# A list order for all of layer 1, and layer 2's first operands summed in DRAM by accumulating transfers

## The chip, the cores and the metric

The kernel runs on one core of a Trainium2 chip. The metric is the device time of one execution in microseconds (us). TensorE multiplies matrices, VectorE and ScalarE do elementwise work, SyncE (SP) issues transfers, and GpSimd (POOL) is idle in the kernel before.

## The reference

Attention with two local masks, then two feed-forward layers over 2304 tokens, all in float32:

```python
scores = np.where(masks, scale * q @ k.T, -1e9)          # 8 heads of 64; heads 4 to 7 dilated by 4
attn = softmax(scores) @ v                               # window of 32 keys, [4, 8, 576, 64]
x = attn.transpose(0, 2, 1, 3).reshape(2304, 512)
h = x @ w_in                                             # layer 1: 512 -> 2048 -> 512
P = a[0] + a[1] * h + a[2] * h**2 + a[3] * h**3
Q = 1 + abs(b[0]) * abs(h) + abs(b[1]) * h**2
y = (P / (Q + 1e-6)) @ w_out
h = y @ w2_in                                            # layer 2: 512 -> 2048 -> 512
out = (max(h, 0) + alpha * min(h, 0)) @ w2_out
```

## The kernel before

**Tiling.** Features lie on partitions. The tokens go in six blocks of 384. In layer 1 a pair `J` (0 to 47, eight to a block) is two chunks of 128 hidden features for one block: `inproj` forms two chunks of `h` in the two PSUM banks `h` (line 645), `rat_1` and `rat_2` evaluate P / Q (lines 663 to 677), `g_split` splits the result into a high part and a low part (lines 684 and 685), and `outproj1` two pairs later multiplies by `w_out` (line 695) and adds up in the banks `y0` to `y3`. Past the first block a product is three matmuls of float32r parts, high times high, high times low and low times high, each of 384 columns. At a block's end `y` goes through a tile `os` to DRAM (`y_dram[block, m]`, m of four groups of 128 features).

**Attention.** A unit `U` (four to a block, the last two dilated) is two heads of one block: scores into banks `aS` and `aP`, a maximum, exponentials (line 512), normalization (line 532), transposes, a copy `pts`, and the product with `v` into a bank `h` (line 582), which is copied as `xh` (line 609) and gives the low part `xl` (line 615). Past the first four, one unit runs in two pairs.

**Layer 2** works on two blocks at a time with seven products in place of eight (Strassen and Winograd). For a block pair, with B11, B21 the first and B12, B22 the second block's halves of y, it needs seven right operands: B11, B21, B22 and T1 = B12 - B11, T3 = B22 - B12, T2 = B22 - T1, T4 = B21 - T2. `x_load` fetches y from DRAM, `x_combine` takes the four differences on VectorE (line 760), and `x_place` splits each operand into a high part on ScalarE (line 742) and a low part on VectorE (line 743). `st_prep` forms and splits the weights' combinations (`st_a`, `st_s`). `product` (line 836) multiplies in the order B11, T2, B21, T3, T4, T1, B22 for each of eight pairs of chunks; `v` and `u` (lines 871 and 866) are the first copies and sums out of the banks. `outproj2` (line 714) gives the output. For the first block pair `x_load(0)` is written at pair 43, `x_combine(0)` and the first `x_place` at 44, and the others at 45 to 47 and behind.

**Weights** arrive as 64-bit numbers and are converted (`w_convert`: ScalarE line 375, VectorE 381 to 396). `w_early` converts eleven tiles of layer 2's during pairs 16 to 42 and writes them back to DRAM (`w_dram`).

**The order.** At its end the program hands all instructions of TensorE, VectorE, ScalarE and SP to `in_order_of_need`. It projects start times with a table of costs, picks on each engine the ready instruction with the longest way to the end, and chains those that it places before `ORDERED`; the rest are left to the framework's scheduler, behind the last chained one:

```python
if start < ORDERED:
    order[e].append(k)
...
rest = [(k, ks[-1]) for k in range(n) if todo[k].engine == e and k not in chosen]
```

`ORDERED` is 115e3 ns, about the first eight pairs. SP stays in written order.

## Time and profile before

| what | us |
|---|---|
| median of 3 runs | 887.02 |
| lowest and highest | 885.96, 888.42 |
| profiled execution, its own time | 887.51 |
| its span, first to last instruction | 885.7 |

The profile is of one execution. Its page gives busy times by engine, the span in slices, the chain of waits that ended last and groups of instructions. The trace behind it answers by stretch of time, by line, and as a timeline. The granted clock of TensorE is 1.0, the upper of its two levels (2.4 GHz), over the whole span. In a timeline the ends of matmuls are modelled and overlap, so starts are compared. A bracket at the end of a row gives the idle time of the engine just before it, and what ended that.

### The profile page before, as it was taken

The numbers are of one execution on the slowest core, as the hardware profiler recorded it, in microseconds if no ns is written. First come the engines' busy times: TensorE is split into PE (matmuls) and PEld (weight loads), VectorE is DVE, ScalarE is ACT, GpSimd is POOL, SyncE is SP. The second block draws the span as 40 slices with busy tenths as digits, with TensorE's granted clock in tenths as the row PEclk, the third lists the DMA queues.
The fourth block names the chain that finished last, engine by engine and source line by source line (L and its number), as shares of the span: only waits on it lengthen the run. The fifth ranks groups of instructions, "written<-read, shape, count | busy, mean of one in ns | idle before, by whom it ended". The sixth has DMA issues, their size and how long they took to land.

```text
span 885.7 us, 14822 instructions
## 1 busy us (share of the span) xinstructions
PE 872.5 (99%) x5746; PEld 779.0 (88%) x5746; DVE 760.7 (86%) x1199; ACT 613.3 (69%) x1253; POOL 0.2 (0%) x4
## 2 busy tenths in 40 slices
PE   9999999999999999999999999999999999999997
PEld 6555678999999999999999999898888989899896
DVE  5999999999999998988899999998986778767652
ACT  6999988788877888887677576557554456635423
POOL 0000000000000000000000000000000000000000
PEclk9999999999999999999999999999999999999999
DMA  9964212133334434440021242323320011210001
GB/s 346 407 238 176 82 57 79 38 115 140 130 109 139 173 125 148 160 149 19 20 78 42 95 131 95 119 79 119 101 85 24 27 46 60 97 47 25 1 0 72
DMA packets 32903, 92.78 MB, mean 105 GB/s; under 512 B 3905, under 2 KB 11329, under 8 KB 32833
## 3 DMA queue, kind: packets, MB, share of 16 engines
q1 hardware_dynamic: 32832, 91.83, 29.9%
q8 instruction: 45, 0.74, 0.3%
q14 instruction: 26, 0.20, 0.1%
HBM read 76.61 MB, written 15.20 MB: 104 GB/s over the span
## 4 chain that ended last, share of the span: by engine, by line
PE 57%; ACT 18%; DVE 18%; DMA 4%; issue 2%; SPq 0%; ACTq 0%
PE ps_h L836 19%; PE ps_y L714 14%; PE ps_y L695 9%; PE ps_h L645 7%; PE ps_aS L714 4%; PE ps_aP L714 3%; ACT p L512 3%; DVE tb L675 2%; DVE tc L676 2%; ACT p L532 2%; ACT tc L664 2%; ACT ta L673 2%; DVE tc L677 2%; ACT ta L674 2%; ACT ta L663 1%
## 5 line engine op out<-in xcount | busy, mean ns | idle before, releaser
L645 PE MATMUL ps_h<-xh,winh 128*128 128x384 f32 x320 | 110.4, 345 | 2.7 <-DVE tc L666 2.2
L695 PE MATMUL ps_y<-gh,wouth 128*128 128x384 f32 x320 | 108.4, 339 | 0.0
L695 PE MATMUL ps_y<-gl,wouth 128*128 128x384 f32 x320 | 107.1, 335 | 0.3 <-DVE gl L685 0.3
L695 PE MATMUL ps_y<-gh,woutl 128*128 128x384 f32 x320 | 107.2, 335 | 0.0
L645 PE MATMUL ps_h<-xh,winl 128*128 128x384 f32 x320 | 107.2, 335 | 0.0
L645 PE MATMUL ps_h<-xl,winh 128*128 128x384 f32 x320 | 107.1, 335 | 0.0
L714 PE MATMUL ps_y<-wouth,gl 128*128 128x512 f32 x192 | 74.9, 390 | 0.0
L714 PE MATMUL ps_y<-woutl,gh 128*128 128x512 f32 x192 | 74.9, 390 | 0.0
L714 PE MATMUL ps_y<-wouth,gh 128*128 128x512 f32 x192 | 74.8, 390 | 0.0
L663 ACT ACTIVATE ta<-ps_h,root 128x384 f32<-128x384 f32 x96 | 57.3, 596 | 18.7 <-PE ps_h L645 18.4
L664 ACT ACTIVATE tc<-ps_h,co 128x384 f32<-128x384 f32 x96 | 66.5, 694 | 0.0
L645 PEld LDWEIGHTS ps_h<-xh,winh 128*128 128x128 f32 x320 | 60.0, 188 | 6.9 <-DVE tc L666 3.7
L742 ACT ACTIVATE gh<-tc 128x768 fp32r<-128x768 f32 x48 | 40.3, 841 | 30.5 <-PE ps_aP L714 28.0
L695 PEld LDWEIGHTS ps_y<-gl,wouth 128*128 128x128 f32 x320 | 60.2, 188 | 0.6 <-DVE gl L685 0.6
L645 PEld LDWEIGHTS ps_h<-xl,winh 128*128 128x128 f32 x320 | 60.1, 188 | 0.3
L743 DVE TENSOR_TENSOR gl<-tc,gh 128x768 fp32r<-128x768 f32 x48 | 45.8, 954 | 16.9 <-ACT gh L742 16.7
L695 PEld LDWEIGHTS ps_y<-gh,wouth 128*128 128x128 f32 x320 | 60.2, 188 | 0.0
L742 ACT ACTIVATE st_a<-w 128x1024 fp32r<-128x1024 f32 x24 | 25.5, 1061 | 50.1 <-PE ps_h L836 41.4
L695 PEld LDWEIGHTS ps_y<-gh,woutl 128*128 128x128 f32 x320 | 60.1, 188 | 0.0
L645 PEld LDWEIGHTS ps_h<-xh,winl 128*128 128x128 f32 x320 | 60.1, 188 | 0.0
L675 DVE SCALAR_TENSOR_TENSOR tb<-tb,ta 128x768 f32<-128x768 f32 x48 | 45.8, 955 | 16.3 <-ACT ta L674 16.0
L666 DVE SCALAR_TENSOR_TENSOR tc<-tc,co,ps_h 128x384 f32<-128x384 f32 x96 | 58.1, 608 | 0.7
(197 smaller groups left out, 2317.8 us busy)
## 6 DMA issues: line engine op xcount, KB each, us to landing
w<-w_dram_in SPq DMA_DIRECT2D x24, 512.0 KB, 3.6
raw<-in_w_in_dram SPq DMA_DIRECT2D x16, 512.0 KB, 5.1
raw_inh<-in_w_out_dram SPq DMA_DIRECT2D x13, 512.0 KB, 3.8
ld_qk<-in_qk_d_dram SPq DMA_DIRECT2D x12, 512.0 KB, 5.0
ld_v<-in_v_d_dram SPq DMA_DIRECT2D x12, 512.0 KB, 4.1
ld_qk<-in_qk_p_dram SPq DMA_DIRECT2D x12, 416.0 KB, 4.2
ld_v<-in_v_p_dram SPq DMA_DIRECT2D x12, 384.0 KB, 3.4
y_dram<-os SPq DMA_DIRECT2D x24, 192.0 KB, 1.9
```

Of the source, the lines that this page charges most:

```text
L512: nc.scalar.activation(out=a["p"][h][:m, t * n:(t + 1) * n], in_=a["s"][h][:m, t * n:(t + 1) * n], func=AF.Exp, scale=scale, bias=a["nm"][ ...
L532: nc.scalar.activation(out=pv, in_=pv, func=AF.Copy, scale=rd[:m, t:t + 1])
L645: nc.tensor.matmul(out=hp[:, :BLK], lhsT=w, rhs=x, start=(k == 0), stop=(k == len(pairs) - 1))
L663: nc.scalar.activation(out=ta, in_=hp, func=AF.Abs, scale=root)
L664: nc.scalar.activation(out=tc_, in_=hp, func=AF.Identity, scale=co[:, 3:4], bias=co[:, 2:3])
L666: nc.vector.scalar_tensor_tensor(out=tc_, in0=tc_, scalar=co[:, 1:2], in1=hp, op0=ALU.add, op1=ALU.mult)
L675: nc.vector.scalar_tensor_tensor(out=tb, in0=tb, scalar=C1, in1=ta, op0=ALU.add, op1=ALU.mult)
L695: nc.tensor.matmul(out=yt[:, :BLK], lhsT=w[:, m * 128:(m + 1) * 128], rhs=g, start=(c == 0 and i == 0), stop=(c == NC - 1 and i == len(pai ...
L714: nc.tensor.matmul(out=yt, lhsT=g[:, tok], rhs=w, start=(first and i == 0), stop=(last and i == 2))
L742: nc.scalar.activation(out=hi, in_=t, func=AF.Copy)
L743: nc.vector.tensor_tensor(out=lo, in0=t, in1=hi.bitcast(F32), op=ALU.subtract)
L836: nc.tensor.matmul(out=hp, lhsT=u[:, ws], rhs=x[:, xs], start=(k == 0), stop=(k == 5))
```

## The change

**The order.** `in_order_of_need` takes a mark `listed`: the instructions written before the second pair of layer 2 (`LISTED = 1`). All of these are chained in the projected order; whatever is written later follows the last instruction that the projection places before `ORDERED`, now 488e3 ns. POOL's transfers are projected like SP's, in written order.

**Operands of the first block pair.** T1 to T4 of it are summed in DRAM. At pair 17 SP copies y into `sum_dram` (`t_begin`). At pairs 18, 20 and 25 `t_minus` loads a half of y into an `os` tile, ScalarE negates it, and a POOL transfer adds it in DRAM. At pair 28 `t_plus` adds one sum to another in DRAM. At pair 43 `x_first` loads B11, T2, B21, T3 and T4 into the tile of their low part. At 44 to 46 `x_lows` copies that to the high part, writes the negated high part over the low tile, both on ScalarE, and lets a POOL transfer add the float32 operand from DRAM: what is left is the low part. T1 and B22 are split as before. `x_combine` is left with the later block pairs.

```diff
+LISTED = 1
-ORDERED = 115e3
+ORDERED = 488e3
...
-        if i.engine in (Engine.PE, Engine.DVE, Engine.Activation, Engine.SP) and (i.ins or i.outs)
+        if i.engine in (Engine.PE, Engine.DVE, Engine.Activation, Engine.SP, Engine.Pool) and any(_is_access(a) for a in i.outs)
...
+    first = {id(i) for i in nc.cur_bb.bb.instructions[:listed]}
...
-        if start < ORDERED:
+        if id(todo[k]) in first:
             order[e].append(k)
+            if start < ORDERED:
+                last[e] = k
...
-        rest = [(k, ks[-1]) for k in range(n) if todo[k].engine == e and k not in chosen]
+        rest = [(k, last[e]) for k in range(n) if e in last and todo[k].engine == e and k not in chosen]
...
+    def t_begin(name, first):
+        for i in range(2):
+            b, j = Y_OF[first]
+            nc.sync.dma_start(out=half(sum_dram[name], i), in_=y_dram[b, 2 * j + i])
+    def t_minus(name, second):
+        for i in range(2):
+            t = ldp.tile([128, DM], F32, tag="os", name="neg")[:, :BLK]
+            b, j = Y_OF[second]
+            nc.sync.dma_start(out=t, in_=y_dram[b, 2 * j + i])
+            nc.scalar.activation(out=t, in_=t, func=AF.Copy, scale=-1.0)
+            nc.gpsimd.dma_start(out=half(sum_dram[name], i), in_=t, accum_op=ALU.add)
+    def t_plus(name, second):
+        nc.gpsimd.dma_start(out=sum_dram[name], in_=sum_dram[second], accum_op=ALU.add)
...
+    def x_first(name):
+        x_alloc(0, name)
+        hi, lo = st_x[0, name]
+        parts = x_of_dram(name)
+        w = 2 * BLK // len(parts)
+        for i, t in enumerate(parts):
+            nc.sync.dma_start(out=lo[:, i * w:(i + 1) * w].bitcast(F32), in_=t)
+        st_s.setdefault(0, {})[name] = lo.bitcast(F32)
+    def x_lows(name):
+        hi, lo = st_x[0, name]
+        parts = x_of_dram(name)
+        w = 2 * BLK // len(parts)
+        nc.scalar.activation(out=hi, in_=lo.bitcast(F32), func=AF.Copy)
+        nc.scalar.activation(out=lo, in_=hi.bitcast(F32), func=AF.Copy, scale=-1.0)
+        for i, t in enumerate(parts):
+            nc.gpsimd.dma_start(out=lo[:, i * w:(i + 1) * w], in_=t, accum_op=ALU.add)
...
+        if J == 17:
+            for name, first in (("T1", "B12"), ("T3", "B22"), ("T4", "B21"), ("T2", "B11")):
+                t_begin(name, first)
...
+        if J == 28:
+            t_plus("T2", "T3")
+            t_plus("T4", "T1")
         if J == NP - 4:
-            x_combine(0)
-            x_place(0, "T2")
+            x_lows("T2")
...
         if J == NP - 3:
             w_next(2)
-            x_place(0, "B11")
-            x_place(0, "B21")
+            x_lows("B11")
+            x_lows("B21")
         if J == NP - 2:
             st_ops = {0: st_prep(0, st_raw.pop(0))}
-            x_place(0, "T3")
-            x_place(0, "T4")
+            x_lows("T3")
+            x_lows("T4")
```

**How the order moves.** Up to about pair 8 it is the same. Three places follow. Lines of the changed kernel are 8 to 58 higher (663 and 664 are 671 and 672 there, 512 is 520, 714 is 722, 836 is 894).

ScalarE at pair 19 of layer 1, a pair with a dilated attention unit: `ta` and `tc` read a bank `h`, once for each half of the pair, and `p` are the exponentials. Before:

```order
L684 ACTIVATE gh<-tc 128x768
L663 ACTIVATE ta<-ps_h,root 128x384
L512 ACTIVATE p,sm<-ps_aS,nm 112x80 x4
L512 ACTIVATE p,sm<-ps_aP,nm 112x80 x4
L664 ACTIVATE tc<-ps_h,co 128x384
L663 ACTIVATE ta<-ps_h,root 128x384
L664 ACTIVATE tc<-ps_h,co 128x384
```

And now:

```order
L671 ACTIVATE ta<-ps_h,root 128x384
L672 ACTIVATE tc<-ps_h,co 128x384
L791 ACTIVATE neg<-neg 128x384 x2
L692 ACTIVATE gh<-tc 128x768
L520 ACTIVATE p,sm<-ps_aS,nm 112x80
L671 ACTIVATE ta<-ps_h,root 128x384
L520 ACTIVATE p,sm<-ps_aS,nm 112x80
L672 ACTIVATE tc<-ps_h,co 128x384
L520 ACTIVATE p,sm<-ps_aS,nm 112x80 x2
L520 ACTIVATE p,sm<-ps_aP,nm 112x80 x4
```

The first half's `ta` and `tc` now stand ahead of all exponentials, and the second half's behind one and two of them; the two negations for T1 have come in between.

ScalarE over the last pair of layer 1, up to the copy `v` of layer 2's first product. Before:

```order
L663 ACTIVATE ta<-ps_h,root 128x384
L664 ACTIVATE tc<-ps_h,co 128x384
L742 ACTIVATE st_T1h<-st_T_5397 128x768
L663 ACTIVATE ta<-ps_h,root 128x384
L664 ACTIVATE tc<-ps_h,co 128x384
L742 ACTIVATE st_B22h<-st_B_5399 128x768
L684 ACTIVATE gh<-tc 128x768
L416 ACTIVATE wouth_5937<-w_5789 128x1024
L673 ACTIVATE ta<-tb,c1t 128x768
L674 ACTIVATE ta<-ta 128x768
L871 ACTIVATE v_5766<-ps_h 128x384
```

And now:

```order
L671 ACTIVATE ta<-ps_h,root 128x384
L672 ACTIVATE tc<-ps_h,co 128x384
L818 ACTIVATE st_T3h<-st_T3l 128x768
L818 ACTIVATE st_T4h<-st_T4l 128x768
L671 ACTIVATE ta<-ps_h,root 128x384
L672 ACTIVATE tc<-ps_h,co 128x384
L750 ACTIVATE st_a<-w_5529 128x1024
L750 ACTIVATE st_s<-st_s 128x768
L692 ACTIVATE gh<-tc 128x768
L819 ACTIVATE st_T3l<-st_T3h 128x768
L819 ACTIVATE st_T4l<-st_T4h 128x768
L929 ACTIVATE v_5807<-ps_h 128x384
```

The first weights' high parts (`st_a`, `st_s`) and the copies and negations of T3 and T4 now stand here. Between these rows and pair 46's last `tc` stand seven more: the copy of T2, the negations of B11 and T2, line 681, the copy of B21, line 682 and the negation of B21. The two splits of layer-2 weights and those of T1 and B22 have moved behind `v`.

TensorE at the first pair of layer 2's second block pair, from the end of its third product, B21, on. Before:

```order
L836 MATMUL ps_h<-st_B21l,st_a 128x384
L836 MATMUL ps_h<-st_B21h,st_a 128x384
L836 MATMUL ps_h<-st_T3h,st_a 128x384
L836 MATMUL ps_h<-st_T3l,st_a 128x384
L836 MATMUL ps_h<-st_T3h,st_a 128x384 x2
```

And now:

```order
L894 MATMUL ps_h<-st_B21h,st_a 128x384
L722 MATMUL ps_y_6081<-wouth_6484,gh 128x512
L722 MATMUL ps_y_6081<-wouth_6484,gl 128x512
L722 MATMUL ps_y_6081<-woutl_6485,gh 128x512
L722 MATMUL ps_aS<-wouth_6484,gh 128x512
L722 MATMUL ps_aS<-wouth_6484,gl 128x512
L722 MATMUL ps_aS<-woutl_6485,gh 128x512
L722 MATMUL ps_aP<-wouth_6484,gh 128x512
L894 MATMUL ps_h<-st_T3h,st_a 128x384
```

Seven matmuls of `outproj2` have moved in between B21's and T3's product.

## Rows read from the trace of the kernel before

**Rows 1.** The page, busy time of each engine, its share and its instructions.

```profile
PE 872.5 (99%) x5746; PEld 779.0 (88%) x5746; DVE 760.7 (86%) x1199; ACT 613.3 (69%) x1253; POOL 0.2 (0%) x4
```

**Rows 2.** Table of stretches: length, then busy us of the engines, clock, DMA share, GB/s.

```profile
20.00:40.00 20.00, 17.41 (x198) 10.92 (x195) 19.06 (x36) 18.92 (x48) 0.00 (x0) 1.00 1.03 406
200.00:250.00 50.00, 49.25 (x440) 47.37 (x438) 47.11 (x75) 40.69 (x97) 0.00 (x0) 1.00 0.40 136
490.00:500.00 10.00, 10.00 (x60) 10.00 (x59) 9.77 (x14) 7.83 (x12) 0.00 (x0) 1.00 0.45 157
```

**Rows 3.** Timeline of TensorE at three stalls: start us, duration, engine, line, operation.

```profile
234.02 0.33 PE L695 MATMUL ps_y<-gl,wouth 128*128 128x384 f32 x1
234.19 0.34 PE L695 MATMUL ps_y<-gh,woutl 128*128 128x384 f32 x1
235.28 0.45 PE L645 MATMUL ps_h<-xh,winh 128*128 128x384 f32 x1 [0.75 <-DVE tc L666]
235.56 0.34 PE L645 MATMUL ps_h<-xl,winh 128*128 128x384 f32 x1
...
312.82 0.34 PE L695 MATMUL ps_y<-gh,woutl 128*128 128x384 f32 x1
313.61 0.45 PE L645 MATMUL ps_h<-xh,winh 128*128 128x384 f32 x1 [0.45 <-DVE tc L666]
...
391.18 0.34 PE L695 MATMUL ps_y<-gh,woutl 128*128 128x384 f32 x1
392.33 0.44 PE L645 MATMUL ps_h<-xh,winh 128*128 128x384 f32 x1 [0.81 <-DVE tc L666]
```

**Rows 4.** Timeline of ScalarE ahead of the first of them.

```profile
229.29 0.56 ACT L663 ACTIVATE ta<-ps_h,root 128x384 f32<-128x384 f32 x1
230.02 0.33 ACT L512 ACTIVATE p<-ps_aS,nm 112x80 f32<-112x80 f32 x1 [0.16 <-DVE nm L496]
...
232.47 0.71 ACT L664 ACTIVATE tc<-ps_h,co 128x384 f32<-128x384 f32 x1
```

**Rows 5.** Timeline of TensorE at two smaller stalls of layer 1.

```profile
171.89 0.44 PE L695 MATMUL ps_y<-gl,wouth 128*128 128x384 f32 x1 [0.26 <-DVE gl L685]
...
425.08 0.44 PE L645 MATMUL ps_h<-xh,winh 128*128 128x384 f32 x1 [0.48 <-DVE xl L615]
```

**Rows 6.** Timeline of TensorE at the first pair of layer 2's second block pair.

```profile
622.48 0.34 PE L836 MATMUL ps_h<-st_T2h,st_s 128*128 128x384 f32 x1
623.23 0.45 PE L836 MATMUL ps_h<-st_B21h,st_a 128*128 128x384 f32 x1 [0.42 <-ACT v L871]
...
624.24 0.34 PE L836 MATMUL ps_h<-st_B21h,st_a 128*128 128x384 f32 x1
624.85 0.44 PE L836 MATMUL ps_h<-st_T3h,st_a 128*128 128x384 f32 x1 [0.28 <-DVE u L866]
```

**Rows 7.** Groups of instructions, 440 to 500 us: busy, mean ns, idle before.

```profile
L743 DVE TENSOR_TENSOR st_T2l<-st_t,st_T2h 128x768 fp32r<-128x768 f32 x1 | 1.0, 952 | 0.0
...
L742 ACT ACTIVATE st_T2h<-st_t 128x768 fp32r<-128x768 f32 x1 | 0.8, 837 | 0.0
```

**Rows 8.** Timeline of ScalarE shortly before the border of the layers.

```profile
456.18 0.92 ACT L673 ACTIVATE ta<-tb,c1t 128x768 f32<-128x768 f32 x1
457.00 1.04 ACT L416 ACTIVATE wouth<-w 128x1024 fp32r<-128x1024 f32 x1
...
486.19 0.67 ACT L664 ACTIVATE tc<-ps_h,co 128x384 f32<-128x384 f32 x1
```

**Rows 9.** Timeline of TensorE across the border of the layers.

```profile
498.00 0.33 PE L836 MATMUL ps_h<-st_B11h,st_a 128*128 128x384 f32 x1
...
503.37 0.33 PE L836 MATMUL ps_h<-st_T3l,st_a 128*128 128x384 f32 x1
```

**Rows 10.** DMA issues by line: count, KB each, median us to landing.

```profile
w<-w_dram_in SPq DMA_DIRECT2D x24, 512.0 KB, 3.6
...
st_B11l<-y_dram SPq DMA_DIRECT2D x6, 192.0 KB, 2.4
```

More of the change, by code (lines that the diff above doesn't have):

```diff
@@ L32 @@
 NARROW = 2.1
+LAG = 2700
 SLACK = 100.0
 FILL = 256
-ORDERED = 115e3
+LISTED = 1
+ORDERED = 488e3
 SIGNED = (('out', 4), ('out', 6), ('out', 8), ('out', 10), ('out', 12))
@@ L133, in _is_filler, with in_order_of_need @@
     return i.engine == mybir.EngineType.PE and _columns(i.outs[0]) == FILL
-def in_order_of_need(tc, nc, places):
+def in_order_of_need(tc, nc, places, listed):
     Engine = mybir.EngineType
@@ L151, in in_order_of_need @@
     holder = {}
-    fixed = {Engine.PE: None, Engine.SP: None}
+    fixed = {Engine.PE: None, Engine.SP: None, Engine.Pool: None}
     size = [0] * n
@@ L158, in in_order_of_need @@
             if fixed[i.engine] is not None:
-                (behind if i.engine == Engine.SP else soft)[k].add(fixed[i.engine])
+                (soft if i.engine == Engine.PE else behind)[k].add(fixed[i.engine])
             fixed[i.engine] = k
@@ L162, in in_order_of_need @@
         writes = [_region(a, places) for a in i.outs if _is_access(a)]
-        if i.engine == Engine.SP:
+        if i.engine in (Engine.SP, Engine.Pool):
             size[k] = writes[0][2] - writes[0][1], (writes[0][4] - writes[0][3])
@@ L210, in in_order_of_need @@
     for k in reversed(range(n)):
-        own = costs[k][1] if todo[k].engine != Engine.SP else 2500 + size[k][0] * size[k][1] / 400
+        own = costs[k][1] if todo[k].engine not in (Engine.SP, Engine.Pool) else 2500 + size[k][0] * size[k][1] / 400
         step = costs[k][0]
@@ L220, in in_order_of_need @@
     ready_at = [0.0] * n
-    free = {Engine.PE: 1300.0, Engine.DVE: 800.0, Engine.Activation: 1500.0, Engine.SP: 730.0}
+    free = {Engine.PE: 1300.0, Engine.DVE: 800.0, Engine.Activation: 1500.0, Engine.SP: 730.0, Engine.Pool: 1300.0}
     waiting = {e: [] for e in free}
@@ L226, in in_order_of_need @@
     order = {e: [] for e in free}
+    last = {}
     landed = 0.0
@@ L256, in in_order_of_need @@
     for e, ks in order.items():
+        if not ks:
+            continue
         chosen = set(ks)
-        rest = [(k, ks[-1]) for k in range(n) if todo[k].engine == e and k not in chosen]
+        rest = [(k, last[e]) for k in range(n) if e in last and todo[k].engine == e and k not in chosen]
         for b, a in [*zip(ks[1:], ks), *rest]:
@@ L766, in x_alloc @@
         ]
+    Y_OF = {"B11": (0, 0), "B21": (0, 1), "B12": (1, 0), "B22": (1, 1)}
+    sum_dram = {name: dp.tile([128, 2 * DM], F32, name=f"sum_dram{name}")[:, :2 * BLK] for name in ("T1", "T2", "T3", "T4")}
+    def t_begin(name, first):
[9 more added lines that the diff above has]
+            nc.gpsimd.dma_start(out=half(sum_dram[name], i), in_=t, accum_op=ALU.add)
@@ new lines, in t_plus, with x_of_dram @@
+    def t_plus(name, second):
+        nc.gpsimd.dma_start(out=sum_dram[name], in_=sum_dram[second], accum_op=ALU.add)
+    def x_of_dram(name):
+        if name in sum_dram:
+            return [sum_dram[name]]
+        b, j = Y_OF[name]
+        return [y_dram[b, 2 * j + i] for i in range(2)]
+    def x_first(name):
[6 more added lines that the diff above has]
+        st_s.setdefault(0, {})[name] = lo.bitcast(F32)
@@ L768, in x_load @@
+    def x_lows(name):
[6 more added lines that the diff above has]
+            nc.gpsimd.dma_start(out=lo[:, i * w:(i + 1) * w], in_=t, accum_op=ALU.add)
     def x_load(n):
-        st = st_s[n] = {}
+        st = st_s.setdefault(n, {})
         if n == 0:
-            for name in ("B11", "B21"):
-                x_alloc(n, name)
-                st[name] = st_x[n, name][1].bitcast(F32)
+            for name in ("B11", "T2", "B21", "T3", "T4"):
+                x_first(name)
+            for name, tag in (("T1", "qk"), ("B22", "v")):
+                st[name] = stage("st_" + name)
+                for i in range(2):
+                    src = half(sum_dram["T1"], i) if name == "T1" else y_dram[1, 2 + i]
+                    nc.sync.dma_start(out=half(st[name], i), in_=src)
+            return
@@ L786, in x_combine @@
         st = st_s[n]
-        if n == 0:
-            st["T2"] = rawp.tile([128, 2 * DM], F32, tag="u", name="st_t2", bufs=1)[:, :2 * BLK]
         sub(st["T1"], st["T3"], st["B11"])
@@ L1071, in attn_rational_prelu_kernel @@
             x_load(0)
+        step = {18: (t_minus, "T1", "B11"), 20: (t_minus, "T3", "B12"), 25: (t_minus, "T4", "B22")}.get(J)
+        if J == 17:
+            for name, first in (("T1", "B12"), ("T3", "B22"), ("T4", "B21"), ("T2", "B11")):
+                t_begin(name, first)
+        if step:
+            step[0](*step[1:])
+        if J == 28:
+            t_plus("T2", "T3")
+            t_plus("T4", "T1")
         if J == NP - 4:
-            x_combine(0)
-            x_place(0, "T2")
+            x_lows("T2")
             w_loads(2, 1)
@@ L1096, in attn_rational_prelu_kernel @@
             k = n * NQ + q
+            if k == LISTED:
+                listed = len(nc.cur_bb.bb.instructions)
             def before():
@@ L1122, in attn_rational_prelu_kernel @@
     out_some(len(todo))
-    in_order_of_need(tc, nc, slots)
+    in_order_of_need(tc, nc, slots, listed)
 def _consts():
```

2 lines of the change are left out of this document (1 added, 1 removed).

## Prediction, made before the changed kernel was run

> **What bounds the kernel now.** I read the page first: TensorE is busy in 872.5 of the 885.7 us of the span [rows 1], so what the change can give lies in the 13 us that are left and in stalls that the busy figure hides. The table of stretches comes next: from 200 to 250 us TensorE is busy in 49.25 of 50 us while VectorE has 47.11; from 490 to 500, at the border of the layers, it is busy in all 10 us, with VectorE at 9.77 [rows 2]. So the border, which the second half of the change rebuilds, has no TensorE time to give back. It can only lose.
>
> The timeline of TensorE shows where layer 1 does lose. Back to back, matmuls of 384 columns start 0.17 us apart (234.02 and 234.19). At 234, 313 and 391 us one starts 1.09, 0.79 and 1.15 us after its predecessor, and the one behind it 0.28 us later, because its weights were not loaded ahead [rows 3]. Over the 0.17 these are 0.92 + 0.62 + 0.98 and three times 0.11: **2.85 us**. All three wait for the `tc` of line 666, which frees the PSUM bank `h`. ScalarE's timeline says why: ahead of the first, `ta` of the pair's first half starts at 229.29, then come the eight exponentials of a dilated attention unit from 230.02, and only at 232.47 the `tc` of that half [rows 4]. That is once in eight pairs, at the first dilated unit of a block, hence the 78 us between the three. Two smaller stalls, 0.26 us for a `gl` at 172 and 0.48 us for an `xl` at 425, have VectorE as releaser [rows 5]. In layer 2 there is one such place, the first pair of the second block pair: 0.75 and 0.61 us between starts, ended by `v` and by `u` [rows 6], or (0.75 - 0.17) + (0.61 - 0.17) + 2 x 0.11 = 1.24 us.
>
> **The list over all of layer 1.** The changed order of ScalarE puts `ta` and `tc` of the first half ahead of the exponentials, and those of the second behind one or two of them. In the old order `tc` stood behind eight, 2.45 us [rows 4]; a delay of two is a quarter of that, 0.6 us, less than the 0.92 by which the first stall is late, and it falls on the second half, whose bank is wanted 12 matmuls (2.1 us) later. I take all three stalls as gone: **-2.85**. The `gl` stall was caused by weight splits that stood ahead of `gl`; the list ranks those lower, but a low-ranked instruction that has started is not interrupted. Between nothing and 0.26 + 0.11 = 0.37 I take **-0.25**, nearer the row. The `xl` stall I leave in: the new order has one more VectorE operation of a weight conversion ahead of that `xl`. Such conversions are now dropped into gaps all along the layer, several of them directly ahead of an `xh`, and each can hold it up by part of its length. Bounds: -0.6 (the stall at 425 also goes) and +2.4 (four of the later units each wait another 0.6, the 0.48 + 0.11 of this row). I take **+0.25**, near the end that has a row.
>
> **The border.** Removed from VectorE are four differences and five low parts of 768 columns, nine times 0.95 us = 8.6 us; added on ScalarE are five negations at 0.84 us [rows 7]. VectorE's 8.6 us are worth nothing in themselves, since TensorE does not wait there [rows 2]. The six negations of 384 columns that form the sums in DRAM cost some 0.6 us each (a `tc` of that size takes 0.67 [rows 8]); they and the SP transfers fall in pairs 17 to 28. There ScalarE has 9 of 50 us free [rows 2], and SP's queue holds operands of a unit that runs two pairs or more later, at 9.8 us a pair (78.4 us for eight [rows 3]): nothing. The sums in DRAM are started at pair 17, finished from pair 28 and read at pair 43; 15 pairs are 147 us, so an accumulating transfer may take ten times as long as any load: nothing.
>
> What remains is the low parts in SBUF, late and in a chain: ScalarE copies, ScalarE negates, a POOL transfer adds. I count it on the old clock. In the new order 17 operations lead from the last `tc` of pair 46, which ends at 486.19 + 0.67 = 486.86 [rows 8], to the negation of T3. Ten of 768 columns at 0.84, two of line 673's kind at 0.92, two `ta` and two `tc` at about 1.25 the two, and `st_a` at 1.04 give 13.8 us; neighbours overlap by 0.1 us (456.18 + 0.92 against 457.00 [rows 8]), so 12.1 us: T3's transfer can be issued at 498.9. TensorE reads T3's low part at 503.37 [rows 9], and the changed order keeps that place. **The margin is 4.4 us.** T4's transfer is issued one operation later and read 18 matmuls later, so T3 decides. No row shows an accumulating transfer. Plain loads of 192 and 512 KB land in 2.4 and 3.6 us [rows 10], so 384 KB takes about 3.1; if the transfer reads both operands one after the other, 2 x 3.6 = 7.2. From the first the stall is 0, from the second 7.2 - 4.4 = +2.8. I stay near the first, since the data of one plain load is the row at hand, and add what is just in time on VectorE (the first weights of layer 2 are now split in the last 3 us before their use): **+0.4**, ends 0 and +2.8. The Trainium skill ("DMA: Bandwidth & Descriptors", Anatomy of one DMA) gives about 2.0 us plus the bytes over 436 GB/s for a POOL transfer, for 384 KB an estimate of 2.9 us; by that the term is 0.
>
> **Behind the border.** At the place of rows 6 the new order has seven layer-2 matmuls between the second and third product; the wait for `u` (0.61 - 0.17 + 0.11 = 0.55) is covered by them. The wait for `v` ahead of the second product stays. **-0.55**, ends 0 and -1.24.
>
> **Sum.** -2.85 - 0.25 + 0.25 + 0.4 - 0.55 = **-3.0 us** on the profiled execution's 887.5 us, that is 884.5; it lies 0.5 above the median of the runs shown, so the forecast is 887.0 - 3.0 = **884.0 us**.
>
> **Rivals.** *Stalls exchanged* (within 0.3%): the three bank stalls go, but conversions ahead of `xh` and `xl` cost what they free, the +2.4 above instead of +0.25. Then 887.0 - 2.85 - 0.25 + 2.4 + 0.4 - 0.55 = 886.2 us. For it: VectorE is 94% busy in layer 1 [rows 2], so a pushed operation finds little room. Against it: the wait for `xl` is one of five stalls in 250 us. It includes the case that the list leaves the exponentials' stalls as they are because the projected times are off.
>
> *The POOL queue takes one transfer at a time* (slower): T2, two of B11, two of B21 and T3 go out in that order, T2 after three ScalarE operations (2.3 us) from 486.86, at 489.1. If each occupies the queue for t, T3's low part is there at 489.1 + 6t. At t = 2.4, the landing of a 192 KB load [rows 10], that is 503.5, in time; at t = 3.6, the 512 KB load, 510.7, or 7.3 us late, and the sum is -3.0 - 0.4 + 7.3 = +3.9: 890.9 us. It is slower by over 0.3% from a stall of 2.7 + 3.4 = 6.1 us, t = 3.4. For it: all of these transfers are issued by one engine, and each was a VectorE operation of 0.95 us [rows 7]. Against it: SP's transfers do overlap; from 20 to 40 us they moved 406 GB/s [rows 2], where 512 KB every 3.6 us would be 146. The Trainium skill ("SBUF — State Buffer", SBUF: two separate sides) has a rule that would bring it about: GpSimd cannot write descriptors while VectorE holds the shared port in a two-port mode. By the same page (Who interferes with whom) it is copies, casts and `tensor_scalar` that do this, and two-input operations don't; no row of this trace shows either.
>
> *VectorE late in layer 2*: the place at 622 is not the only wait behind the border: two weight splits and the low parts of T1 and B22 now stand behind the first `u`, four operations of some 0.95 us [rows 7]. If TensorE, which had no wait from 490 to 500 [rows 2], waited for all of them, the last term were +3.8 instead of -0.55: 887.0 - 2.45 + 3.8 = 888.4 us, also within 0.3%.
>
> **Chances.** The measurement of this kernel can tell about 0.3%, 2.7 us, from no change. My forecast and what lies below it, faster: 0.47. Within 0.3%, by exchanged stalls, by a later layer 2 or by a border that costs 1 to 3 us: 0.36. Slower, by the POOL queue 0.14 and by the rest 0.03: 0.17. Cases of both signs hold most of the chance: the forecast's own range is 881.5 to 885.0. The low end of the whole is every stall gone and a free border, -2.85 - 0.37 - 0.6 - 1.24 = -5.1, and 0.9 for the spread of the runs: 881.0. The high end leaves out the last of the POOL rival: 889.5.
>
> **What would show it.** Right: no stall on line 674's `tc` in the waits; TensorE starting layer 2's first product about 3 us earlier than 498.00; no wait of T3 or B21 for a DMA. Wrong: TensorE or its weight load waiting for a DMA into `st_T3l`, `st_B11l` or `st_B21l` (the POOL rival); new waits for `xl` or `gl` (exchanged stalls); TensorE idle between 500 and 540 for `u` or `v` (VectorE late). If the starts at the three places are 0.17 us apart and the time is still 887, the loss is behind the border.

## The result and the profile after

| | us |
|---|---|
| changed kernel, median of 5 runs | 894.88 (892.27 to 897.26) |
| kernel before, median of 5 runs | 887.44 (885.96 to 890.99) |
| ratio, 95% interval | 1.0081 (1.0059 to 1.0103) |
| profiled execution, its span | 892.27, 890.5 |

The change makes the kernel 0.8% slower. The profiled execution is the fastest of the five; its difference to the profiled one of before, 4.8 us of span, is what the rows below account for. The medians differ by 7.4 us; the other 2.6 us lie in executions that have no trace.

TensorE waits in new places. Its stalls of [rows 3] at 313 and 391 us are gone, and the one at 234 is 0.37 in place of 0.75 us, the first row below. Here are four of those it has now, in TensorE's timeline of the changed kernel (start us, duration, line, operation; in brackets the idle time and what ended it):

```profile
236.48 0.45 PE L653 MATMUL ps_h<-xh,winh 128*128 128x384 f32 x1 [0.37 <-DVE tc L674]
...
249.33 0.45 PE L653 MATMUL ps_h<-xh,winh 128*128 128x384 f32 x1 [0.77 <-DVE xl L623]
...
301.76 0.44 PE L703 MATMUL ps_y<-gh,wouth 128*128 128x384 f32 x1 [0.30 <-ACT os L709]
...
506.44 0.45 PE L894 MATMUL ps_h<-st_T3l,st_a 128*128 128x384 f32 x1 [1.09 <-DMA st_T3l<-sum_dramT]
```

The last is the first product of T3, and it waits for a DMA. ScalarE's timeline around the first stall, the place of [rows 4]:

```profile
228.31 0.67 ACT L672 ACTIVATE tc<-ps_h,co 128x384 f32<-128x384 f32 x1
230.52 0.53 ACT L791 ACTIVATE neg<-neg 128x384 f32<-128x384 f32 x1 [1.55 <-DMA neg<-y_dram]
232.13 0.53 ACT L791 ACTIVATE neg<-neg 128x384 f32<-128x384 f32 x1 [1.08 <-DMA neg<-y_dram]
232.56 0.83 ACT L692 ACTIVATE gh<-tc 128x768 fp32r<-128x768 f32 x1
```

ScalarE stands 2.6 us for the loads of two tiles that it is to negate, and the rest of the pair stands behind. SP's own timeline shows what stands ahead of these loads: the eight copies that begin the sums.

```profile
220.74 5.75 SPq L783 DMA_DIRECT2D sum_dramT<-y_dram  x8
226.54 1.06 SPq L790 DMA_DIRECT2D neg<-y_dram  x2
```

At the border SP is late by far more. Before, the last write-back of an early converted weight and the loads of layer 2's first operands stood here:

```profile
383.07 0.79 SPq L739 DMA_DIRECT2D st_T<-y_dram  x2
...
389.13 0.49 SPq L360 DMA_DIRECT2D w_dram_in<-win  x1
...
393.96 0.80 SPq L739 DMA_DIRECT2D st_B11l<-y_dram  x2
402.82 0.80 SPq L739 DMA_DIRECT2D st_B<-y_dram  x2
...
452.43 0.80 SPq L739 DMA_DIRECT2D st_B21l<-y_dram  x2
```

and in the changed kernel:

```profile
454.89 0.87 SPq L364 DMA_DIRECT2D raw<-in_w_in_dram  x2
477.03 0.33 SPq L368 DMA_DIRECT2D w_dram_in<-win  x1
479.65 0.80 SPq L810 DMA_DIRECT2D st_B11l<-y_dram  x2
480.56 0.36 SPq L810 DMA_DIRECT2D st_T2l<-sum_dramT  x1
481.02 0.85 SPq L810 DMA_DIRECT2D st_B21l<-y_dram  x2
481.92 0.42 SPq L810 DMA_DIRECT2D st_T3l<-sum_dramT  x1
```

The list keeps SP in written order, and the loads are written behind the last early conversion, which it leaves until 477.03. Before, only the first 115 us were chained, and the scheduler could move SP's transfers behind that. The table of stretches over the border, beside [rows 2]:

```profile
480.00:490.00 10.00, 10.00 (x59) 10.00 (x58) 8.51 (x12) 7.50 (x11) 0.00 (x0) 1.00 0.91 291
490.00:500.00 10.00, 10.00 (x59) 9.61 (x57) 7.52 (x14) 10.00 (x16) 4.40 (x5) 1.00 0.92 251
500.00:510.00 10.00, 8.62 (x46) 7.66 (x46) 9.71 (x13) 5.71 (x8) 1.86 (x3) 1.00 0.96 220
```

The DMA engines are over 90% busy, and ScalarE 10.00 of 10 us. The queues and landings from 486 to 510 us (q0 is POOL's, all of it accumulating; for the queues packets, MB and share of the DMA engines' time; for the landings KB each and median us to landing):

```profile
q0 software_dynamic: 1008, 1.97, 47.9%
q1 hardware_dynamic: 1949, 4.25, 47.1%
...
st_T2l<-sum_dramT POOLq DMA_DIRECT2D x1, 384.0 KB, 7.1
st_B11l<-y_dram POOLq DMA_DIRECT2D x2, 192.0 KB, 7.7
st_B21l<-y_dram POOLq DMA_DIRECT2D x2, 192.0 KB, 4.5
st_T3l<-sum_dramT POOLq DMA_DIRECT2D x1, 384.0 KB, 6.0
st_T4l<-sum_dramT POOLq DMA_DIRECT2D x1, 384.0 KB, 7.8
```

An accumulating transfer lands after 4.5 to 7.8 us here, and its megabyte takes 2.2 times the engines' time of a plain one (47.9 / 1.97 against 47.1 / 4.25).

### The profile page after: what moved, and what is told of

Its sections match the earlier page's. It is cut to its first block, busy times and chain, and to the rows that moved or that the text cites. A ratio compares the mean times of both kernels' runs of the same rounds, so it can differ in the third digit from the quotient of the medians.

```text
span 890.5 us, 14881 instructions
## 1 busy us (share of the span) xinstructions
PE 876.8 (98%) x5746; PEld 780.0 (88%) x5746; DVE 751.6 (84%) x1190; ACT 618.6 (69%) x1264; POOL 13.6 (2%) x19
## 3 DMA queue, kind: packets, MB, share of 16 engines
q0 software_dynamic: 2160, 3.93, 2.6%
## 4 chain that ended last, share of the span: by engine, by line
PE 65%; ACT 13%; DVE 12%; DMA 5%; issue 3%; SPq 1%; POOL 0%; ACTq 0%; DVEq 0%; POOLq 0%
PE ps_h L894 18%; PE ps_y L722 14%; PE ps_y L703 12%; PE ps_h L653 11%; PE ps_aP L722 3%; PE ps_aS L722 3%; ACT p L520 2%; ACT ta L681 2%; ACT p L540 2%; ACT ta L682 2%; DVE tc L684 1%; ACT tc L672 1%; PE ps_h L590 1%; DVE tb L683 1%; ACT ta L671 1%
```

## The experiments

The table splits each run's span, less that of before, by TensorE's start times: up to the 61st `inproj` matmul (60.09 us before; the order is nearly the same there, and profiled executions differ by up to 2.6 us), from there to the 961st (450.85), from there to the 85th `product` matmul, where layer 2's third pair begins (527.09), and to the end. Medians are of 4 to 12 runs. A row's four parts are of one execution and need not add up to the difference of the medians. The changed kernel and runs 3, 4 and 11 have nearly the same order in layer 1 and lie between -0.58 and 0.26 there, so differences under 1 us say nothing.

| run | median us | ratio to before (95%) | start | layer 1 | border | rest |
|---|---|---|---|---|---|---|
| the change | 894.88 | 1.0081 (1.0059, 1.0103) | 1.33 | -0.29 | 4.15 | -0.42 |
| 1 order alone | 893.92 | 1.0064 (1.0046, 1.0082) | -0.07 | -3.63 | 8.20 | -0.46 |
| 2 operands alone | 896.23 | 1.0091 (1.0072, 1.0110) | 0.61 | 5.44 | 2.46 | -0.15 |
| 3 lows on VectorE | 892.19 | 1.0051 (1.0035, 1.0067) | 0.17 | 0.26 | 2.85 | 0.27 |
| 4 next loads late | 894.85 | 1.0082 (1.0064, 1.0100) | 0.24 | -0.58 | 7.10 | 0.50 |
| 5 chain to 400 us | 893.56 | 1.0068 (1.0053, 1.0082) | 1.39 | -3.25 | 8.69 | -0.74 |
| 6 order, lead | 898.82 | 1.0120 (1.0106, 1.0134) | 2.36 | 1.51 | 6.91 | 0.56 |
| 7 negations later | 892.61 | 1.0055 (1.0042, 1.0068) | 0.23 | -2.46 | 5.31 | 1.28 |
| 8 lead | 894.13 | 1.0077 (1.0061, 1.0092) | 0.15 | 5.07 | 0.77 | -0.17 |
| 9 sooner, negations later | 891.98 | 1.0053 (1.0032, 1.0073) | -0.15 | 3.86 | 0.07 | -1.10 |
| 10 order, sooner | 887.97 | 0.9996 (0.9980, 1.0012) | 1.39 | -4.18 | 3.50 | 1.15 |
| 11 POOL farther | 892.08 | 1.0044 (1.0030, 1.0058) | 0.22 | -0.04 | 2.91 | 0.17 |
| 12 negations on GpSimd | 891.08 | 1.0031 (1.0019, 1.0043) | -0.14 | -3.97 | 5.44 | -0.05 |
| 13 the same, sooner | 892.63 | 1.0048 (1.0032, 1.0065) | 2.57 | 3.68 | 0.16 | -1.02 |
| 14 the same, last five sooner | 894.81 | 1.0077 (1.0062, 1.0092) | -0.15 | 6.45 | 0.30 | -1.00 |
| 15 order, sooner, lows by transfer | 885.65 | 0.9975 (0.9961, 0.9988) | 0.41 | -3.93 | 2.63 | -0.37 |

### Runs 1 to 4: the parts

Run 1 is the kernel before with the new `in_order_of_need` (the first part of the diff of the change, and nothing of the second):

```diff
+LISTED = 1
-ORDERED = 115e3
+ORDERED = 488e3
...
-        if start < ORDERED:
+        if id(todo[k]) in first:
```

Run 2 is the changed kernel with the old one:

```diff
-ORDERED = 488e3
+ORDERED = 115e3
...
-        if id(todo[k]) in first:
+        if start < ORDERED:
```

Run 3 takes the five low parts on VectorE:

```diff
-            x_lows("T2")
+            x_place(0, "T2")
```

and so for B11, B21, T3 and T4. Run 4 orders the loads `late` of `x_load(1)` behind the last SP transfer written ahead of them:

```diff
+                        for i in late:
+                            if n == 0 and id(i) not in kept:
+                                tc.add_manual_dep(
+                                    i, anchor.name,
...
```

> The list over all of layer 1 with the operands of before: no sums in DRAM, no transfer on POOL, low parts on VectorE. Theory (the loss sits in the accumulating low parts at the border; the list itself is about neutral): the three stalls at 234, 313 and 391 us go, but the new ones that the changed kernel shows at 236 to 248 us, at 300 and at 380 (outproj1 behind os, products behind pts and tc, together some 2.5 us) come in their place, so layer 1 ends within 1 us of before; no TensorE wait for a DMA into a low part; 886 to 888.5 us. Rival (the list is what is slow): layer 1 ends 2 us or more later than before and the time is 890 us or more, also without POOL. Second rival (the list gains its 2.85 us when the negations are not among ScalarE's work): layer 1 ends about 2.5 us earlier and the time is 884 to 885 us.

> The operands of the changed kernel with the old order (chained up to 115 us, the framework's scheduler behind it). ScalarE's copies and negations of T3, T4, B11 and T2 then stand many operations earlier, two pairs or more ahead of the border, only B21's stay near it. Theory (the low parts are late because copy, negation and transfer follow each other in the last 10 us): T2, T3, T4 and B11 are in time, at most B21's is late, the three stalls of layer 1 stay, and the time is 886.5 to 888.5 us, as before. Rival (the accumulating transfers cost time wherever they stand, by the DMA engines they occupy or by other loads that they delay): 890 us or more, with waits for a DMA at the border or for weights behind it.

> The changed kernel with the five low parts of layer 2's first operands taken by VectorE as before (subtract in place), the sums T1 to T4 still made in DRAM. Five negations (4.2 us of ScalarE) and seven transfers on POOL go, five operations of 0.95 us on VectorE come. Theory (late accumulating transfers): the four waits for a DMA behind 499 us, 0.16 + 0.36 + 1.26 + 0.26 = 2.0 us, go, and what follows in the second pair (1.6 us) goes at least in part: 2 to 3.5 us below the changed kernel, 891.5 to 893 us beside its median of 894.9. Rival (VectorE is what is late at the border): VectorE has 4.8 us more to do there and the time stays at 894 us or above.

> The changed kernel, but the four loads of T3 and B22 of the second block pair (192 KB each), which SP issues at 488.2 to 490.8 us, wait behind a weight load of some 90 us later; nothing else moves. Theory (at the border the DMA engines are full, 92% busy from 490 to 500 us, and the low parts queue behind these 768 KB): at some 390 GB/s they take 2.0 us of all engines; T3's accumulation lands in 4 to 5 us in place of 6.0, the wait for it shrinks from 1.1 to 0 - 0.3 us, and the time falls by 1 to 2 us. Rival (an accumulating transfer takes its 6 to 7 us by itself): T3's landing stays at 6 us, the wait stays, and the time is unchanged within 0.5 us.

Run 1 met none of its three sides whole: it gained in layer 1 as the second rival had it, and was as slow as the first. The list alone wins 3.6 us in layer 1, more than the three stalls, and loses 8.2 at the border without one transfer on POOL. The table of stretches of before, and of run 1, 200 to 400 and 400 to 510 us:

```profile
200.00:400.00 200.00, 197.99 (x1652) 191.48 (x1650) 184.79 (x297) 164.67 (x417) 0.00 (x0) 1.00 0.42 141
400.00:510.00 110.00, 109.52 (x716) 108.44 (x716) 102.42 (x144) 75.26 (x127) 0.00 (x0) 1.00 0.16 51
```

```profile
200.00:400.00 200.00, 199.76 (x1716) 193.26 (x1714) 173.88 (x282) 161.36 (x411) 0.00 (x0) 1.00 0.34 116
400.00:510.00 110.00, 105.83 (x634) 102.99 (x627) 103.88 (x149) 73.54 (x128) 0.00 (x0) 1.00 0.28 96
```

From 200 to 400 us VectorE does 184.79 - 173.88 = 10.9 us less: conversions of layer 2's weights, which the list puts off. They meet the nine operand operations at the border. The largest waits there are 1.09 us for a `tc` and 1.71 us for a `ta`, both of VectorE.

Run 2: the rival, for another reason than its own. No wait for a DMA is at its border, but ScalarE stands 3.26 and 2.84 us ahead of two negations, and TensorE stands behind it (the last row):

```profile
228.86 0.52 ACT L785 ACTIVATE neg<-neg 128x384 f32<-128x384 f32 x1 [3.26 <-DMA neg<-y_dram]
...
232.60 0.53 ACT L785 ACTIVATE neg<-neg 128x384 f32<-128x384 f32 x1 [2.84 <-DMA neg<-y_dram]
...
239.47 0.44 PE L647 MATMUL ps_h<-xh,winh 128*128 128x384 f32 x1 [2.54 <-DVE tc L668]
```

Run 3: 2.7 us below the changed kernel's median, as the theory had it, but 2.85 us of the border remain: waits for `v` (0.40) and `gh` (0.56), the weight loads behind them, and late starts for which the profile names no cause.

Run 4: the theory fell. Without these 768 KB T3's low part lands no sooner (7.3 us); the DMA engines are 93% busy from 480 to 500 us all the same. And TensorE's timeline in this execution shows what a late one can cost:

```profile
503.13 0.34 PE L894 MATMUL ps_h<-st_T3h,st_a 128*128 128x384 f32 x1
506.32 0.51 PE L894 MATMUL ps_h<-st_T3l,st_a 128*128 128x384 f32 x1 [2.85 <-DMA st_T3l<-sum_dramT]
506.62 0.84 PE L894 MATMUL ps_h<-st_T3h,st_a 128*128 128x384 f32 x2
507.26 0.52 PE L894 MATMUL ps_h<-st_T3l,st_a 128*128 128x384 f32 x1
```

Behind the wait matmuls start 0.32 us apart in place of 0.17, until 509.82: TensorE at its lower level, 1.2 GHz. The stretch from 500 to 510 us has a granted clock of 0.83, and the slower starts sum to 1.7 us on top of the wait. In the changed kernel's profiled execution the wait was 1.09 us and the clock stayed at 1.0; its four other runs have mean clocks of 0.997 to 0.999 and take 2.5 to 5.0 us longer. That the lower clock stands behind a late T3 there too is likely, and not shown.

### Runs 5 to 8: where the loss enters

Run 5 is the kernel before with one number changed:

```diff
-ORDERED = 115e3
+ORDERED = 400e3
```

Runs 6 (on run 1) and 8 (on the changed kernel) rank write-backs higher, with `LEAD = 30e3`:

```diff
+        if todo[k].engine == Engine.SP and todo[k].outs[0].bass_ap.tensor.name.startswith("w_dram"):
+            own += LEAD
```

Run 7 lets the projection take longer for the loads of the negated tiles:

```diff
+            if _is_access(todo[k].outs[0]) and todo[k].outs[0].bass_ap.tensor.name.startswith("neg"):
+                done += 6000
```

> The kernel before with one number changed: the chain ends at 400 us in place of 115 us; operands as before, no transfer on POOL, and from 400 us on the framework's scheduler orders the border. Theory (the list is right for layer 1, and what it loses it loses at the border, where SP in written order issues the loads of layer 2's first operands at 476 to 479 us in place of 394 to 452 us): layer 1 ends 2.5 to 3.5 us earlier than before, the border costs under 1 us, 884 to 885 us. Rival (VectorE carries the postponed weight conversions over the border whoever orders it): the border loses 3 us or more again, 887 us or above.

> The list with the operands of before, as in the run of the order alone, but the write-back of each early converted weight of layer 2 counts as 30 us farther from the end, so that the conversions are not left till last and SP comes to the loads behind them earlier. Theory (the border's 7.3 us come from these loads, held up in SP's written order by the last write-back at 473.05 us): the loads are issued at 452 to 460 us, the differences and low parts on VectorE start 15 us earlier or more, the border loses 0 to 3 us in place of 7.3, and the time is 884.5 to 888 us. Rival (VectorE is too full from 480 to 510 us for nine operand operations, wherever their loads stand): the border loses 5 us or more, 890 us or above.

> The changed kernel, but the list counts the loads of the tiles that are negated as landing 6 us later, so that the six negations stand later on ScalarE; the border is as in the changed kernel. Theory (ScalarE stands 1.55 and 1.08 us at 229 to 232 us waiting for these loads, and what is queued behind, gh, exponentials, ta and tc, is late by as much): no idle time of ScalarE above 0.5 us ahead of a negation, no stalls at 235.8 to 248.2 us, layer 1 ends 1.5 to 2.5 us earlier than in the changed kernel, and the time falls by as much, to 892.5 to 893.5 us. Rival (the accumulating transfers in DRAM delay the loads of attention): the stalls of layer 1 stay, 894 to 896 us.

> The changed kernel with the same 30 us for the write-backs of early converted weights; sums, negations and accumulating low parts as in the changed kernel. Theory (the low parts are late because the loads they start from are issued at 479.7 us, behind the write-backs in SP's written order): the loads are issued by 460 us, copies and negations stand earlier on ScalarE, the transfers of T3 and T4 land before TensorE reads them, the border loses 0 to 2 us in place of 4.1 or more, no half clock behind a wait for T3, 889 to 891.5 us. Rival (the accumulating transfers are late by themselves, 6 to 9 us from issue to landing, and follow one another): the wait for T3 stays, 894 us or above.

Run 5: the rival by its number. The postponed conversions are done later here too, the last write-back at 452.79 us, and TensorE waits 3.70 us for a `gl` at 481: on VectorE three differences and a low part stand ahead of it, from 473 to 480 us. Behind the wait starts are 0.32 us apart until 485. Run 6: the rival; the loads moved by 4 us only (471.40), since the last conversion's own loads stand behind four writes of y, and layer 1 is 5 us later than in run 1. Run 7: the theory; the stalls at 236 to 248 us go, layer 1 gains 2.2 us on the changed kernel, and a new wait of 1.13 us comes at 300. Run 8 is right about the border, 0.77 us with no wait for a DMA, though its loads came at 472.69 and not by 460; it is wrong about the sum, since layer 1 is 5.4 us later than in the changed kernel. In both runs most of that lies in one place: at 423 us VectorE is at the raised conversion, TensorE waits 2.0 us ahead of an attention product, and behind it runs at 1.2 GHz (starts 0.32 us apart) until 429 and 431 us.

### Runs 9 to 11: the border

Runs 9 (on run 7) and 10 (on run 1) write the eleven early conversions sooner; run 11 is the changed kernel with a higher rank for what leads to a POOL transfer (`POOL_MORE = 6e3`).

```diff
-        if J >= NC and early and (J - NC) * 5 // 13 > (J - NC - 1) * 5 // 13:
+        if J >= NC and early and J % 2 == 0:
```

```diff
+        if todo[k].engine == Engine.Pool:
+            own += POOL_MORE
```

> The changed kernel with two places altered: the eleven early conversions are written at every second pair from 16 to 36 in place of 16 to 42, and the loads of the negated tiles count as landing 6 us later, as in the run before. Theory (SP's written order holds the first loads of layer 2 behind the last early conversion, whose own loads in turn stand behind the block's four writes of y at 444 to 451 us): the last write-back is done by 440 us, the loads of layer 2's first operands are issued at 451 to 455 us, no TensorE wait for a DMA at the border, border cost under 1 us, layer 1 ends 1 to 2.5 us earlier than in the kernel before; 884.5 to 887 us. Rival (conversions written sooner crowd layer 1, as with the 30 us lead, where layer 1 lost 5 us): 889 us or above, with the loss ahead of 450 us.

> The list with the operands of before and the early conversions at every second pair from 16 to 36. Theory (the order alone lost 7.3 us at the border because VectorE's nine operand operations and the postponed conversions met there, the loads coming at 475 us): the loads come at about 452 us, the nine operations spread from 455 us on, the border costs 0 to 2 us, layer 1 keeps most of its 2.8 us: 884.5 to 887.5 us. Rival (the list leaves operand operations until they are needed, whenever their loads come, and VectorE is full there): the border costs 4 us or more again, 889 us or above.

> The changed kernel, but a transfer on POOL counts 6 us more toward the end in the list's ranking; T3's and B21's negations then stand ahead of the first weights' high parts on ScalarE; the loads stay where they are, at about 479 us. Theory (lateness of the negations is what TensorE waits for, and the loads at 479 us leave room for it): T3's transfer is issued 3 us earlier or more, its wait falls from 1.1 to 2.9 us to under 0.5 us, the border costs 1 to 2.5 us in place of 4.1 to 7.6; 890.5 to 892.5 us. Rival (with loads as late as that the transfers are late in any order, since each takes 6 us or more): a wait of 1 us or more for T2, B21 or T3 stays, 893.5 us or above.

Run 9 has its loads at 456.04 us and POOL's transfers from 465.78 on; its border costs 0.07 us. So the same transfers, issued 25 us sooner, are free. Conversions and loads moved together here, so the run alone does not part them; but VectorE was busier from 480 to 500 us than in the changed kernel (19.97 against 16.03 us), which speaks for the late loads. Its layer 1 went to the rival. Run 10 met its theory in layer 1, and at the border in the loads (449.52) but not in the cost (3.50 us; VectorE still 20.00 of 20 us busy from 480 to 500): 6 us below run 1 for one line. Run 11 met its theory but for the border, 2.91 us in place of 1 to 2.5: with T3's transfer issued at 496.89 no wait for a DMA is left, though the loads stay where they were (T3's at 479.14); what remains are waits for `tc`, `v` and `gl`. T3's negation was done at 491.17 already; the transfer went out 0.30 us after B11's second had landed (the last section).

### Runs 12 to 15: the two causes taken away

```diff
-            nc.scalar.activation(out=t, in_=t, func=AF.Copy, scale=-1.0)
+            nc.gpsimd.tensor_scalar(out=t, in0=t, scalar1=-1.0, scalar2=None, op0=ALU.mult)
```

Run 12 is the changed kernel with this; run 13 adds the sooner conversions of run 9, run 14 only the last five of them sooner:

```diff
-        if J >= NC and early and (J - NC) * 5 // 13 > (J - NC - 1) * 5 // 13:
+        if J in (16, 19, 22, 24, 27, 29, 31, 33, 35, 37, 39):
```

Run 15 is run 10 with `x_place` for B11, B21, T2, T3 and T4 of the first block pair ending in

```diff
-        split(*st_x[n, name], st_s[n][name])
+            nc.scalar.activation(out=hi, in_=t, func=AF.Copy)
+            nc.scalar.activation(out=lo, in_=hi.bitcast(F32), func=AF.Copy, scale=-1.0)
+            nc.gpsimd.dma_start(out=lo, in_=t, accum_op=ALU.add)
```

(for B11 and B21 from `y_dram`, in halves).

> The changed kernel with the six negations of 384 columns on GpSimd in place of ScalarE; every transfer stays. Theory (ScalarE's waits for the loads of the negated tiles make the stalls at 236 to 248 us and push the copies behind them): no such stalls, layer 1 ends 2 to 3 us earlier than in the kernel before, start aside, the border loses 3 to 7 us as in the changed kernel; 891 to 893 us. Rival (the transfers are what delays layer 1): layer 1 ends within 1 us of before and the stalls at 236 to 248 us stay; 894 us or above.

> The changed kernel with the negations on GpSimd and the early conversions at every second pair from 16 to 36. Theory (ScalarE's waits in layer 1 and the late loads at the border are the two whole causes of the loss): layer 1 ends 2.5 to 4 us earlier than in the kernel before, start aside, the border costs under 1 us, no wait for a DMA there, 883.5 to 885.5 us, below both kernels. Rival (a third cost goes with the sums or the list): 887 us or above, and the place where it lies is then seen in the products' start times.

> The changed kernel with the negations on GpSimd, and of the eleven early conversions the last five written at pairs 31, 33, 35, 37, 39 in place of 32, 35, 37, 40, 42; up to pair 29 all as in the changed kernel. Theory (the two causes are the whole loss): layer 1 ends 2.5 to 4 us earlier than in the kernel before, start aside, the loads of layer 2's first operands are issued by 460 us, no TensorE wait for a DMA at the border, border cost under 1.5 us: 883.5 to 886 us. Rival (conversions written sooner always cost layer 1 what they give at the border): layer 1 loses 2 us or more between 330 and 450 us, 887.5 us or above.

> The run of the order with sooner early conversions, with one alteration: the low parts of B11, B21, T2, T3 and T4 come by copy, negation and an accumulating transfer on POOL (of y in DRAM, or of the difference's tile), and no longer from VectorE; the four differences stay on VectorE, nothing is summed in DRAM. Theory (at the border VectorE's time is what is short, and a transfer issued by 480 us is in time): five operations of 0.95 us leave VectorE, layer 1 is as in that run, the border costs 0 to 2 us in place of 3.4, no wait for a DMA: 885 to 887 us, beside 888.0 of that run. Rival (ten operations of 0.84 us on ScalarE in place of five delay v and the weights there by as much): the border costs 3 us or more, 888 us or above.

Run 12: the theory. With every transfer in place, but ScalarE free of the negations, layer 1 goes from -0.29 to -3.97 us: the waiting engine, not the transfers, cost 3.7 us. Runs 13 and 14 confirm the border (0.16 and 0.30 us) and go to their rivals in layer 1. Run 14 loses 9 us between 375 and 390 us, where VectorE and TensorE show how:

```profile
376.44 0.69 DVE L389 TENSOR_SCALAR win<-win 128x1024 uint32<-128x1024 uint32 x1 [2.56 <-ACT win L383]
377.17 1.29 DVE L399 SCALAR_TENSOR_TENSOR win<-raw,win 128x512 uint32<-128x512 uint32 x2
...
379.58 0.95 DVE L683 SCALAR_TENSOR_TENSOR tb<-tb,ta 128x768 f32<-128x768 f32 x1
...
382.71 0.61 DVE L674 SCALAR_TENSOR_TENSOR tc<-tc,co,ps_h 128x384 f32<-128x384 f32 x1
```

```profile
378.59 0.29 PE L466 MATMUL ps_aS<-msk 64*64 64x320 bf16 x1 [1.90 <-ACT pts L576]
...
383.38 1.55 PE L590 MATMUL ps_h<-pts,ld_v 96*64 96x64 f32 x24 [3.31 <-DVE tc L674]
```

VectorE stands 2.56 us for ScalarE's step of a conversion (`win`), works on it until 379.6, and only then comes to the `tb` and `tc` of the pair, which free the bank `h`; ScalarE takes its two steps ahead of `pts`. TensorE waits 1.90 and 3.31 us, and from 370 to 390 us the granted clock is 0.74.

Yet sooner conversions alone do not cost layer 1: run 10 has those of run 13, without the sums, and gains 4.18 us. SP's timelines of run 13 (first) and of run 10 differ here by the eight copies, and a conversion's own loads (`raw`) and write-back come later behind them:

```profile
221.99 5.80 SPq L783 DMA_DIRECT2D sum_dramT<-y_dram  x8
227.83 1.06 SPq L364 DMA_DIRECT2D raw<-in_w_out_dram  x2
242.86 0.33 SPq L368 DMA_DIRECT2D w_dram_out<-wout  x1
```

```profile
220.81 0.94 SPq L364 DMA_DIRECT2D raw<-in_w_out_dram  x2
236.77 0.33 SPq L368 DMA_DIRECT2D w_dram_out<-wout  x1
```

From 238 to 250 us run 13 loses 3.6 us. That the copies on SP cause it is argued from these rows and was not tried. No run of the sums has both the gain in layer 1 and a free border.

Run 15 is faster than both kernels: 2.3 us below run 10, 0.25% below the kernel before, and no stall of TensorE above 0.15 us from 377 to 512 us. Its border's 2.63 us come behind that, as waits for a `gh` (0.33) and a `gl` (1.37).

## Why the prediction was wrong, step by step

The forecast was -3.0 us, the profiled execution shows +4.8. Of the 7.8 us between them 2.6 lie in layer 1, 3.8 at the border and 1.3 in the start, where the order is nearly the same.

**"I take all three stalls as gone: -2.85"** is right for the list by itself: runs 1, 12 and 15 gain 3.6 to 4.0 us in layer 1. The small `gl` stall is gone as well; the `xl` stall at 425 stayed, as the prediction left it. In the changed kernel only 0.29 us of this are left.

**"The six negations ... nothing"** failed first. The step counted their 0.6 us and ScalarE's free share. It did not count that what is chained behind a negation waits with it until the loaded tile has landed (1.55 and 1.08 us of ScalarE), nor that on SP eight copies stand ahead of the two loads. Runs 7 and 12, with the negations later and off ScalarE, gain 2.2 and 3.7 us in layer 1.

**"I count it on the old clock"** was right about ScalarE's chain and wrong about what follows. From the last `tc` of pair 46 to the end of T3's negation it took 499.95 - 488.05 = 11.9 us, predicted 12.1:

```profile
487.39 0.66 ACT L672 ACTIVATE tc<-ps_h,co 128x384 f32<-128x384 f32 x1
...
499.10 0.85 ACT L819 ACTIVATE st_T3l<-st_T3h 128x768 fp32r<-128x768 f32 x1
```

T3's transfer was to be issued at 498.9; it was at 500.36, with the chain starting 1.2 us later than on the old clock, and at 498.98 in run 4. Its landing was taken as 3.1 us with 7.2 as the far end; it measured 6.0 and 7.3, and in run 4 the wait is 2.85 us, the far end. The page cited ("DMA: Bandwidth & Descriptors" of the Trainium skill, Anatomy of one DMA) gave an estimate of 2.9 us, by a fit that does not speak of accumulation; no accumulating transfer of 384 KB came under 4.1 us in any run read for this, so the trace disagrees. The term held T3 alone: the changed kernel also waits for B21 and T4, and in the pair after for `v`, `gh` and `gl`. Nor did it hold the lower clock behind such a wait (1.7 us in run 4).

**The step that the prediction left out** is where the loads come. It took the landing from plain loads at other times and did not ask what stands ahead of these on SP. The list ranks by the way to the end, so the conversions, needed late in layer 2, were put off by up to 88 us (389.13 to 477.03), and SP's written order put the loads behind them. ScalarE did find its operands landed, T3's at 488.17; but loads and accumulating transfers then shared DMA engines that were over 90% busy from 480 us on, and the copies and negations had no room to stand earlier. Runs 8, 9, 13 and 14, with loads 7 to 24 us sooner, lose 0.07 to 0.77 us at the border.

**"VectorE's 8.6 us are worth nothing in themselves"** holds for the order of before. Under the list with the operands of before VectorE is full at the border, and in run 15, with five operations less there than run 10, the border costs 0.87 us less (the medians differ by 2.3 us).

**"-0.55" for the wait for `u`** came near by luck: the stretch behind the border gave -0.42. The wait for `v`, which the prediction left in, is gone, and ahead of T3's product 0.48 us between starts are left of 0.61. But in four earlier pairs T3's first matmul, now behind `outproj2`, starts 0.27 us after its predecessor and the next 0.28 us later, in place of 0.17. In the other runs this column scatters from -1.10 to 1.28.

The rivals were all partly there: the stalls exchanged (layer 1), the POOL queue (in another form, below), VectorE late (run 1). None alone gives 894.88, and their sum was not considered.

## What to carry to other kernels

A list that ranks by the longest way to the end puts off what is due late, and an in-order queue passes that delay to whatever is written behind: for each such queue, ask what its next urgent transfer stands behind. An instruction on a busy engine that reads a fresh load costs the wait of that engine, not its own length; give it to an idle engine or leave a distance. Accumulating transfers do take work off VectorE, if they are issued well ahead of their use: 15 us and more was in time in runs 8, 9 and 15, 6 to 8 us was not in the changed kernel and run 4.

## What the runs showed of the hardware

POOL's queue held three transfers in flight. In none of the runs was a fourth issued before the first had landed. POOL's timeline of the changed kernel:

```profile
490.65 0.92 POOL L821 DMA_DIRECT2D st_T2l<-sum_dramT  x1 [172.49 <-ACT st_T2l L819]
491.44 1.94 POOL L821 DMA_DIRECT2D st_B11l<-y_dram  x2
498.04 0.89 POOL L821 DMA_DIRECT2D st_B21l<-y_dram  x1 [4.65 <-ACT st_a L750]
499.22 0.89 POOL L821 DMA_DIRECT2D st_B21l<-y_dram  x1 [0.29 <-issue]
500.36 0.88 POOL L821 DMA_DIRECT2D st_T3l<-sum_dramT  x1 [0.25 <-issue]
```

T2 lands at 490.65 + 7.1 = 497.7, and B21's first half goes out at 498.04, though ScalarE had written it by 493.3; the releaser named is not the one. In runs 4 and 9 the landings are at 494.42 and 471.88, the fourth issues at 494.72 and 472.18. T3 is sixth, so it waits for the third to land as well as for its negation; here both came at 499.9. What sets the number three was not tried.

TensorE's granted clock fell behind single waits: to 0.83 from 500 to 510 us behind the 2.85 us of run 4, to 0.83 from 480 to 490 us behind the 3.70 us of run 5, and to 0.53 from 424 to 431 us behind the 2.01 us of run 8. Behind 2.54 us in run 2 and 1.74 us in run 12 it stayed at 1.00. So the length of the last wait alone does not decide it.

The start differs by up to 2.6 us between profiled executions of kernels whose order is nearly the same there. In runs 6 and 13, the two latest, 1.5 us of it come from the lower clock (granted 0.69 and 0.74 from 35 to 40 us). Up to 1.4 us are there by the first wait at 21 to 23 us in several runs, the changed kernel among them; why stays open.
